# Merging all stages of a gated convolution and attention kernel by a list scheduler in its source

## The chip, the cores and the metric

The kernel runs on one core of one Trainium2 chip. The metric is the time on the device in microseconds (us), from the first to the last instruction of the core. A core has TensorE for matrix products (PE in the profile, with its weight loads as a row of their own, PEld), VectorE (DVE), ScalarE (ACT), GpSimd (POOL), a queue that mostly starts transfers (SP), and 16 DMA engines. TensorE writes only to PSUM, an accumulator memory of 128 partitions with 8 banks of 512 fp32 columns each; VectorE or ScalarE has to carry every result from there to the on-chip working memory. Below, this is called an eviction.

## The reference

There are two branches over the same input x of 2048 positions and 640 channels, mixed by one gate per position. Branch A is a short causal convolution of k with 4 taps, multiplied by v, and then a causal convolution as long as the sequence, done with Fourier transforms. Branch B is an attention in which each position looks at itself and at seven earlier ones, two positions apart; 32 heads have 20 channels each.

```python
x = A_q
g = _sigmoid((x * gate_w).sum(-1, keepdims=True))

# branch A
for t in range(4):
    k_shift = k_shift + k_pad[:, t:t + S, :] * shift_k[:, 3 - t]
kv = k_shift * v
y = irfft(rfft(pad(kv)) * rfft(pad(ssm_k)))[:S]       # length 2 * S
y = y + kv * ssm_D
a = x * y

# branch B
q, k, v = split_heads(x @ wqkv)                       # 32 heads of 20
idx = pos[:, None] - 2 * arange(8)[None, :]           # window of 8, dilation 2
attn = softmax(where(idx >= 0, q . k[idx] * scale, -1e9))
b = (attn @ v[idx]) @ wo

out = g * a + (1 - g) * b
```

All inputs and the output are bf16. The transform is written as matrix products in two steps forward (`s1`, `s2`), a product of spectra, and two steps backward (`i1`, and `i2` with the table T).

## The kernel before

The stages stand one after another in the source, with hand-written interleaving: each stage is a generator, and the main loop advances one or another of them by so many steps. Each stage opens PSUM pools of its own.

In the head x is transposed, v is projected, and VectorE computes the short convolution. Its result goes to a scratch tensor in DRAM, because it is computed with 16 consecutive positions in each partition and the transform needs another layout.

```python
def load_kv(c):
    ...
    if c == 0:
        nc.gpsimd.memset(kh[0:1, 0:3, :], 0.0)
        nc.sync.dma_start(kh[1:128, 0:3, :], raw(k2, 13 * D, [[16 * D, 127], [D, 3], [1, D]]))
    eng.dma_start(kh[:, 3:7, :], raw(k2, t0 * D, [[16 * D, 128], [D, 4], [1, D]]))
    eng.dma_start(vn[:, t0:t0 + 4, :], raw(v2, t0 * D, [[16 * D, 128], [D, 4], [1, D]]))
...
load_x(0); load_w(2); load_x(1)
...
load_kv(0)
load_x(2); load_x(3)
load_w(0); load_w(1)
load_kv(1)
...
            nc.gpsimd.dma_start(raw(kvs, 4 * c * 80, [[16 * 80, 128], [S * 80, 8], [1, 320]]),
                                pr[:, 2].rearrange("p (u m) -> p u m", u=8))
```

The projections of q and k are evicted to a staging tile `stg`, and small transfers ("fragments") of 4 to 20 partitions each sort their rows into the sets of four heads (`qb`, `kb`) that attention uses. There are three sets, used in turn.

Attention runs over 8 groups of four heads, each in 10 halves: scores (`sc`), exp on ScalarE into one of six tiles `ET`, product with v (`O`), division on VectorE. The rest of the projection, and then the transform of the filter for the first three of five channel groups, are slotted in.

```python
for s in range(len(halves)):
    if s + 1 < len(halves):
        scores(s + 1)
    ...
    if 6 <= s < 36:
        advance(qk, 1)
    if s == 20:
        load_h()
    if s == 37:
        ...
        hg = h_early()
    if hg is not None and s % 5 != 4:
        advance(hg, 1)
    advance(kvg, 1)
    pv(s)
kv = p0.tile([128, 2, 64, 80], BF, name="kv", tag="Kslot")
... # kv is read back from its scratch in DRAM
```

Then come the transform of kv, the remaining filter groups, the spectral products, the first inverse step, and, between them, the output projection of attention. Each block of it is scaled by 1 - g and written to a second scratch tensor, which is read back in the layout of the last step:

```python
            for n0, n1 in ((0, 512), (512, 640)):
                for ft in range(NDT):
                    nc.tensor.matmul(opf[:, n0:n1], lhsT=oT[:, ft, :], rhs=wo[:, ft, n0:n1], ...)
            ... # fin = (1 - g) * op, on ScalarE or VectorE
            for r0, n, dst in pos_rows(b_scr, BP * b, BP):
                nc.gpsimd.dma_start(dst, fin[r0:r0 + n, :])
...
    if k == 60:
        qg = p0.tile([128, 16, D], BF, name="qg", tag="Hslot")
        ... # q is loaded
        bl = p0.tile([128, 16, D], BF, name="bl", tag="Kslot")
        ... # b_scr is read back
T = p2.tile([128, 64, 2, 32], BF, name="T", tag="Am", bufs=2)
nc.sync.dma_start(T[:], cf["T"].ap().rearrange("p (a r b) -> p a r b", a=64, r=2))
for t in range(16):
    nc.vector.tensor_scalar(qg[:, t, :], qg[:, t, :], g_nat[:, t:t + 1], None, ALU.mult)
for t0 in range(0, 16, 3):
    ... # i2 = last inverse step on TensorE
    ... # qg = i2 * qg, four parts; qg = qg + bl; qg is stored
```

Of the kernel before, what the change touches and what calls it, by code (L numbers as in the profile page):

```python
# [31 lines left out]
NT = 8  # L32
KW = 128 * NB
QW = BP * NB
GROUPS = [[0, 1, 2, 3], [4, 5, 6, 7], [8, 9, 10], [11, 12, 13], [14, 15, 16]]

# [65 lines left out]
def pos_rows(x2, p0, n):  # L102
    out = []
    for par in range(2):
        a, b = max(p0, HS * par), min(p0 + n, HS * par + S // 2)
        if a < b:
            v = x2.rearrange("(e two) d -> two e d", two=2)
            out.append((a - p0, b - a, v[par, a - HS * par:b - HS * par, :]))
    return out


class Load:
    def __init__(self, nc):
        self.nc = nc
        self.t = dict(a=0.0, d=0.0)

    def pick(self, n):
        ca, cd = n * 0.833 + 80, n * 1.042 + 70
        if self.t["a"] + ca <= self.t["d"] + cd:
            self.t["a"] += ca  # L120
            return "a"
        self.t["d"] += cd
        return "d"

    def copy(self, dst, src, n, eng=None):
        eng = eng or self.pick(n)
        if eng == "a":
            self.nc.scalar.copy(dst, src)  # L128
        else:
            self.nc.vector.tensor_copy(dst, src)  # L130


def advance(gen, n):
    for _ in range(n):
        if next(gen, "end") == "end":
            return False
    return True
# [3 lines left out]
def kernel(  # L141
# [18 lines left out]
    dpool = ctx.enter_context(tc.tile_pool(name="scratch_dram", bufs=1, space=DRAM))  # L160
    b_scr = dpool.tile([S, D], BF, name="b_scr")
    kv_scr = dpool.tile([8, S, 80], BF, name="kv_scr")
    g_scr = dpool.tile([S], F32, name="g_scr")
    cf = {k: nc.inline_tensor(v, name=f"cf_{k}") for k, v in fft_consts().items()}
    ca = {k: nc.inline_tensor(v, name=f"ca_{k}") for k, v in attn_consts().items()}
    ld = Load(nc)
# [3 lines left out]

    p0 = ctx.enter_context(tc.tile_pool(name="p0", bufs=1))
    ident = p0.tile([128, 128], BF, name="ident")
    xS = p0.tile([128, 16, D], BF, name="xS", tag="A")
    vn = p0.tile([128, 16, D], BF, name="vn", tag="Hslot")
# [3 lines left out]
    g_sb = p0.tile([128, 16], F32, name="g_sb")  # L178
    g_nat = p0.tile([128, 16], F32, name="g_nat")
    omg = p0.tile([128, NB], F32, name="omg")  # L180
    oTs = []
    for e in range(3):
        oTb = p0.tile([128, NDT, 128], BF, name=f"oT{e}")
        oTs.append(oTb)

    sA = ExitStack()
    pA = sA.enter_context(tc.tile_pool(name="pA", bufs=1, side="right", reuse_waits="tile"))
    VWs = [p0.tile([128, NB, H // 2, 21], BF, name="VWa", tag="VWa"), pA.tile([128, NB, H // 2, 21], BF, name="VWb")]
    valid = pA.tile([128, NB], BF, name="valid")
    ksets, qsets, ETs = [], [], []  # L190
    for e in range(3):
        kb = pA.tile([128, KW], BF, name=f"kb{e}")
        qb = pA.tile([128, QW], BF, name=f"qb{e}")
        ksets.append(kb); qsets.append(qb)
    NET = 6
    for e in range(NET):
        ETb = pA.tile([128, 2, 512], BF, name=f"ET{e}")
        ETs.append(ETb)
    sB = ExitStack()
    p1 = sB.enter_context(tc.tile_pool(name="pB", bufs=1, side="right", reuse_waits="tile"))  # L200
    sC = ExitStack()
    pC = sC.enter_context(tc.tile_pool(name="pC", bufs=1, side="left", reuse_waits="tile"))
    xT = pC.tile([128, NDT, XW], BF, name="xT")
    W = pC.tile([128, NDT, 3, D], BF, name="W")
    wg = pC.tile([128, NDT], BF, name="wg")
    wl = pC.tile([128, 4, D], BF, name="wl")

# [3 lines left out]
    khs = [None] * 4  # L211

    def load_x(c):
        nc.sync.dma_start(xS[:, 4 * c:4 * c + 4, :], xq4[:, c // 2, 4 * (c % 2):4 * (c % 2) + 4, :])

    def load_w(w):
        nc.sync.dma_start(W[:, :, w, :], W3[:, :, w, :])

    def load_kv(c):
        kh = p1.tile([128, 7, D], BF, name="kh", tag="kh", bufs=2)  # L220
        khs[c] = kh
        t0 = 4 * c
        eng = nc.sync if c < 2 else nc.gpsimd
        if c == 0:
            nc.gpsimd.memset(kh[0:1, 0:3, :], 0.0)
            nc.sync.dma_start(kh[1:128, 0:3, :], raw(k2, 13 * D, [[16 * D, 127], [D, 3], [1, D]]))
        eng.dma_start(kh[:, 3:7, :], raw(k2, t0 * D, [[16 * D, 128], [D, 4], [1, D]]))
        eng.dma_start(vn[:, t0:t0 + 4, :], raw(v2, t0 * D, [[16 * D, 128], [D, 4], [1, D]]))

    nc.sync.dma_start(ident[:], ca["ident"].ap())  # L230
    for c0, c1 in ((0, PRE), (HS, HS + PRE), (2 * HS, XW)):
        nc.gpsimd.memset(xT[:, :, c0:c1], 0.0)
    load_x(0); load_w(2); load_x(1)
    wraw = p1.tile([128, D, 4], BF, name="wraw", tag="stg", bufs=2)
    nc.gpsimd.dma_start(wraw[:], raw(A_shift_k, 0, [[0, 128], [4, D], [1, 4]]))
    nc.gpsimd.dma_start(valid[:], ca["valid"].ap())
    nc.gpsimd.dma_start(wg[:], gate_w.rearrange("(t p) -> p t", p=128))
    load_kv(0)
    load_x(2); load_x(3)
    load_w(0); load_w(1)  # L240
    load_kv(1)
    nc.gpsimd.memset(Dz[:], 0.0)
    nc.gpsimd.memset(omg[:], 0.0)
    for e in range(NET):
        nc.gpsimd.memset(ETs[e][:], 0.0)
    for e in range(3):
        nc.gpsimd.memset(oTs[e][:], 0.0)
    for e in range(2):
        nc.gpsimd.tensor_copy(VWs[e][:, :, :, DH], valid[:].unsqueeze(2).to_broadcast([128, NB, H // 2]))

    def load_feats(e):
        for h4 in range(4):
            nc.sync.dma_start(ksets[e][32 * h4 + DH:32 * h4 + DH + NF, :], ca["mk"].ap())
            nc.sync.dma_start(qsets[e][32 * h4 + DH:32 * h4 + DH + NF, :], ca["mq"].ap())

    load_feats(0)
    for q in range(4):
        nc.gpsimd.dma_start(Dz[32 * q:32 * q + 1, :], A_ssm_D[160 * q:160 * q + 160].unsqueeze(0))
    nc.gpsimd.dma_start(F1b[:], cf["F1b"].ap())
    nc.gpsimd.dma_start(M[:], cf["M"].ap().rearrange("p (a b) -> p a b", a=2))  # L260


    kvs = kv_scr[:]

    def kv_gen():
        nc.vector.tensor_copy(wl[:], wraw[:].rearrange("p c j -> p j c"))
        pr = p0.tile([128, 4, 4 * D], BF, name="pr", tag="Kslot")
        yield
        for c in range(4):
            kh = khs[c]  # L270
            if c:
                nc.vector.tensor_copy(kh[:, 0:3, :], khs[c - 1][:, 4:7, :])
            for j in (0, 1, 3, 2):
                nc.vector.tensor_tensor(pr[:, j].rearrange("p (n c) -> p n c", n=4), kh[:, 3 - j:7 - j, :],  # L274
                                        wl[:, j, :].unsqueeze(1).to_broadcast([128, 4, D]), ALU.mult)
                yield
            nc.vector.tensor_tensor(pr[:, 0:2], pr[:, 0:2], pr[:, 2:4], ALU.add)
            yield
            nc.vector.tensor_tensor(pr[:, 0], pr[:, 0], pr[:, 1], ALU.add)
            nc.vector.tensor_tensor(pr[:, 2].rearrange("p (u n i) -> p n u i", u=8, n=4),  # L280
                                    pr[:, 0].rearrange("p (n u i) -> p n u i", n=4, u=8),
                                    vn[:, 4 * c:4 * c + 4, :].rearrange("p n (u i) -> p n u i", u=8), ALU.mult)
            nc.gpsimd.dma_start(raw(kvs, 4 * c * 80, [[16 * 80, 128], [S * 80, 8], [1, 320]]),
                                pr[:, 2].rearrange("p (u m) -> p u m", u=8))
            if c < 2:
                load_kv(c + 2)
            yield

    kvg = kv_gen()


    pv_ = ExitStack()
    ppv = pv_.enter_context(tc.tile_pool(name="ppv", bufs=2, space=PSUM, reuse_waits="tile"))

    def transposes(c):
        for d0 in (0, 2, 4):
            nd = min(2, NDT - d0)
            tr = ppv.tile([128, 2, 4, 128], BF, name="trx", tag="trx")
            for dd in range(nd):
                for k in range(4):  # L300
                    nc.tensor.transpose(tr[:, dd, k, :], xS[:, 4 * c + k, 128 * (d0 + dd):128 * (d0 + dd) + 128], ident[:, :])  # L301
            ld.copy(xT[:, d0:d0 + nd, ccol(4 * c):ccol(4 * c) + 512],
                    tr[:, 0:nd].rearrange("p d k c -> p d (k c)"), 512 * nd, eng="a")

    def vproj(b):
        ps = ppv.tile([128, 1024], F32, name="psv", tag="psv")
        for n0, n1 in ((0, 512), (512, 640)):
            for dt in range(NDT):
# [28 lines left out]
    def qk_gen(engs):  # L337
        for ft in range(NDT):
            for which in range(2):
                stg = p1.tile([128, KW], BF, name="stg", tag="kh" if ft >= 2 and which else "stg", bufs=2)  # L340
                wd = BP if which == 0 else 128
                for c in range(5):
# [12 lines left out]
                    if c < 4:  # L355
                        yield
# [358 lines left out]
```

The softmax here doesn't subtract the row's maximum and nothing guards it: scores larger than these inputs give would overflow.

## Time and profile before

| | |
|---|---|
| median of three runs | 355.84 us (353.16 to 358.53) |
| span of the profiled execution | 354.1 us |
| busy: PE, DVE, ACT, POOL | 254.6, 211.4, 165.9, 41.2 us |
| first score, last product of attention | 86 us, 212 us |
| last matmul of the first inverse step | 318.8 us |
| first matmul of the last step | 329.9 us |
| moved by DMA | 46.37 MB, mean 131 GB/s |

A line of groups or of the timeline names the line of the source, the engine, the operation and the tiles, as output<-input, with a time in us and the number of instructions. What stands in brackets in the timeline is how long the engine was idle before, and whom it waited for. A line of the chain of waits gives a start, a length and what filled it. A line of the windows view gives, for a stretch of the span, its length, the busy time of PE, PEld, DVE, ACT and POOL with the number of instructions, the granted clock of TensorE as a share of full speed, the share in which the DMA engines were busy, and GB/s. A DMA on the SP queue is shown by the time of its issue; when it landed is seen in who waited for it.

### The profile page before, as it was taken

To read this page: it belongs to the slowest core of one execution; us is meant where nothing else is said; L and a number is where in the kernel's file an instruction comes from. 1 tells how busy PE (TensorE), PEld (TensorE's weight loads), DVE (VectorE), ACT (ScalarE), POOL (GpSimd) and SP (SyncE) were. 2 spreads that over 40 slices of the span, in tenths; PEclk is the share of its full clock that TensorE was granted. 3 is DMA by queue.
4 is the path that set the end of the run, shared out by engine and by line. 5 is a ranking of instruction groups with operands and counts; after the bars stand their busy time and mean duration, and the time that the engine had idled before them with its cause. 6 is when DMAs were issued, how large, how long until landed. Compare 5 with 4: busy or idle time off the path is not lost. (4 is left out here: it accounts for less than half of the span.)

```text
span 354.1 us, 9846 instructions
## 1 busy us (share of the span) xinstructions
PE 254.6 (72%) x4355; PEld 174.0 (49%) x4355; DVE 211.4 (60%) x295; ACT 165.9 (47%) x239; POOL 41.2 (12%) x67
## 2 busy tenths in 40 slices
PE   2760599958779999857877888898989488660430
PEld 2330355524336655545655655575657477660320
DVE  1400999692836565857776633844574668671595
ACT  3250264525526555634545585756565577531000
POOL 8910023010150000000000000112111000000000
PEclk9995599999659999755555556999999968867555
DMA  7375854974441499761891019217121507999165
GB/s 200 137 241 178 267 151 118 211 199 102 103 84 31 88 168 163 193 191 30 181 213 51 4 27 217 65 41 170 39 54 38 138 4 164 213 213 212 57 149 132
DMA packets 34603, 46.37 MB, mean 131 GB/s; under 512 B 23757, under 2 KB 28572, under 8 KB 33152
## 3 DMA queue, kind: packets, MB, share of 16 engines
q1 hardware_dynamic: 31088, 35.77, 42.9%
q0 software_dynamic: 2896, 8.66, 9.3%
q10 hardware_dynamic: 576, 1.31, 1.6%
q8 instruction: 34, 0.56, 0.7%
q14 instruction: 9, 0.07, 0.1%
HBM read 27.19 MB, written 7.87 MB: 99 GB/s over the span
## 5 line engine op out<-in xcount | busy, mean ns | idle before, releaser
L421 ACT ACTIVATE ET<-sc 128x726 bf16<-128x726 f32 (+1 forms) x80 | 67.1, 858 | 57.8 <-PE sc L418 57.2
L352 PE MATMUL pj<-xT,W 128*128 128x484 bf16 (+3 forms) x250 | 55.9, 368 | 6.2 <-ACT stg L128 4.0
L274 DVE TENSOR_TENSOR pr<-kh,wl 128x2560 bf16<-128x2560 bf16 x16 | 23.0, 1487 | 28.2 <-DMA kh<-in_A_k_dram 23.4
L485 PE MATMUL s<-Am,G 64*128 64x64 bf16 x1280 | 29.2, 206 | 13.9 <-DVE Hs L130 4.1
L352 PEld LDWEIGHTS <-W 128*128 128x128 bf16 x250 | 21.7, 102 | 29.8 <-issue 11.9
L418 PE MATMUL sc<-qb,kb 31*128 31x121 bf16 x544 | 36.0, 260 | 0.6 <-issue 0.6
L485 PEld LDWEIGHTS <-G 64*128 64x128 bf16 x1280 | 26.1, 105 | 17.9 <-issue 12.1
L435 PEld LDWEIGHTS <-ET 128*128 128x128 bf16 x544 | 22.4, 102 | 20.8 <-ACT ET L421 9.3
L618 PE MATMUL op<-wo,oT 128*128 128x128 bf16 (+1 forms) x170 | 27.3, 310 | 4.3 <-ACT oT L128 3.5
L130 DVE CAST stg<-pj 128x484 bf16<-128x484 f32 (+3 forms) x30 | 17.9, 598 | 20.8 <-PE pj L352 16.2
L130 DVE CAST Am<-s 128x512 bf16<-128x512 f32 x36 | 23.4, 686 | 11.5 <-PE s L468 9.9
L309 PE MATMUL psv<-W,xT 128*128 128x128 bf16 (+1 forms) x170 | 27.6, 327 | 2.8 <-DMA W<-in_B_wqkv_dram 2.8
L525 PE MATMUL i<-M,Hw 128*128 128x128 bf16 x160 | 25.6, 253 | 4.9 <-DVE Hw L513 2.6
L525 PE MATMUL i<-M,Hs 128*128 128x128 bf16 x160 | 26.0, 253 | 4.1 <-DVE Hs L512 4.1
L626 POOL DMA_DIRECT2D b_scr<-fin x18 | 9.6, 531 | 161.7 <-DVE fin L624 137.9
L128 ACT CAST Am<-s 128x512 bf16<-128x512 f32 x44 | 23.6, 610 | 6.7 <-PE s L468 4.6
L525 PEld LDWEIGHTS <-Hs 128*128 128x128 bf16 x160 | 22.5, 154 | 7.0 <-DVE Hs L512 4.5
L130 DVE CAST Hs<-s 128x1024 bf16<-128x1024 f32 x15 | 18.4, 1224 | 11.7 <-PE s L485 11.7
L301 PE MATMUL trx<-ident,xS 128*128 128x128 bf16 x80 | 7.9, 265 | 22.6 <-DMA xS<-in_A_q_dram 20.4
L525 PEld LDWEIGHTS <-Hw 128*128 128x128 bf16 x160 | 22.4, 155 | 3.0 <-DVE Hw L513 3.0
L128 ACT CAST Cm<-i 128x1024 bf16<-128x1024 f32 x15 | 15.2, 1012 | 15.9 <-PE i L525 15.7
L309 PEld LDWEIGHTS <-xT 128*128 128x128 bf16 x170 | 14.7, 106 | 15.4 <-issue 7.2
(73 smaller groups left out, 362.5 us busy)
## 6 DMA issues: line engine op xcount, KB each, us to landing
Hw<-Hs SPq DMA_DIRECT2D x10, 512.0 KB
xS<-in_A_q_dram SPq DMA_DIRECT2D x4, 640.0 KB
kv_scr<-pr POOLq DMA_DIRECT2D x4, 640.0 KB, 5.4
h_lin<-in_A_ssm_k_dram SPq DMA_DIRECT2D x8, 320.0 KB
kv<-kv_scr SPq DMA_DIRECT2D x4, 640.0 KB
qg<-in_A_q_dram SPq DMA_DIRECT2D x4, 640.0 KB
bl<-b_scr SPq DMA_DIRECT2D x4, 640.0 KB
W<-in_B_wqkv_dram SPq DMA_DIRECT2D x3, 800.0 KB
```

The costliest lines, as they stand in the source:

```text
L128: self.nc.scalar.copy(dst, src)
L130: self.nc.vector.tensor_copy(dst, src)
L274: nc.vector.tensor_tensor(pr[:, j].rearrange("p (n c) -> p n c", n=4), kh[:, 3 - j:7 - j, :], wl[:, j, :].unsqueeze(1).to_broadcast([128, ...
L309: nc.tensor.matmul(ps[:, n0:n1], lhsT=xT[:, dt, BP * b:BP * b + 128], rhs=W[:, dt, 2, n0:n1], start=(dt == 0), stop=(dt == NDT - 1))
L352: nc.tensor.matmul(ps[:, 0:n], lhsT=W[:, dt, which, 128 * ft:128 * ft + 128], rhs=rhs, start=(dt == 0), stop=(dt == NDT - 1))
L418: nc.tensor.matmul(sc[:, hh, BP * bb:BP * bb + BP], lhsT=kb[r:r + DH + NF, 128 * b:128 * b + 128], rhs=qb[r:r + DH + NF, BP * b:BP * b + B ...
L421: nc.scalar.activation(ETs[s % NET][:, :, 0:nw], sc[:, :, 0:nw], ACT.Exp, scale=SCALE)
L435: nc.tensor.matmul(O[:, sl * 21:sl * 21 + 21], lhsT=ET[:, hh, BP * bb:BP * bb + 128], rhs=VWs[t // 4][:, b, 4 * (t % 4) + 2 * hf + hh, :], ...
L485: nc.tensor.matmul(o, lhsT=st["G"][rows, j, r, :], rhs=Am[rows, 2 * j + r, :, :], start=(r == 0), stop=(r == 1), tile_position=(64 * c, 0) ...
L525: nc.tensor.matmul(o, lhsT=src[:, c, :, :, 8 * oc + il].rearrange("p q j -> p (q j)"), rhs=M[:, k, :], start=(k == 0), stop=(k == 1), skip ...
L618: nc.tensor.matmul(opf[:, n0:n1], lhsT=oT[:, ft, :], rhs=wo[:, ft, n0:n1], start=(ft == 0), stop=(ft == NDT - 1))
L626: nc.gpsimd.dma_start(dst, fin[r0:r0 + n, :])
```

## The change

The interleaving by hand is replaced by a list scheduler that runs while the kernel is built. Each stage is a stream that yields requests: which engines may do it, a guessed duration, what it depends on, how many PSUM slots it takes or gives back. The scheduler picks the request that can start earliest, with a small penalty by priority, books it, and lets the stream emit its instructions. What is built is one fixed order for each engine. All stages share one ring of four PSUM slots of two banks each. An eviction that either ScalarE or VectorE may do goes to the one that would be done first.

Both scratch tensors for data go. k and v are loaded with 160 channels of 64 positions a partition, which is the layout of the transform, so kv never leaves the chip. The output projection multiplies weight tiles of 32 positions, so that its result comes out in the layout of the last step and stays on chip. The product of q with the gate moves from VectorE to GpSimd, and q and T are loaded as soon as their places are free. The core of the diff:

```diff
-class Load:
-    def pick(self, n):
...
+class Plan:
+    def start(self, r, e):
+        t = self.at[e]
+        for d in r.deps:
+            if d.t is None:
+                return INF
+            t = max(t, d.t + LAT.get((d.eng, e), 60.0))
+        if r.take:
+            free = sorted(s.free.t + 120.0 if s.free.t is not None else INF for s in self.slots)
+            t = max(t, free[r.take - 1])
...
+    def run(self):
+        while self.streams:
+            for k, (pri, gen, r) in enumerate(self.streams):
+                end, st, e = self.best(r)
...
+                key = (st + 120.0 * p, p, k)
...
-    b_scr = dpool.tile([S, D], BF, name="b_scr")
-    kv_scr = dpool.tile([8, S, 80], BF, name="kv_scr")
+    plan = Plan(4)
...
+        def load_kv(a):        # after load_x(0), Wv, load_x(1..3)
+            dk = [ev(f"conv{a - 2}")] if a >= 2 else []
+            dv = [ev(f"conv{a - 1}")] if a >= 1 else []
+            for q in range(4):
+                yield from load(f"k{a}{q}", kin[a % 2][32 * q:32 * q + 32, lo:19, :],
+                                raw(k2, n0 * D + 160 * q, [[64 * D, 32], [D, 19 - lo], [1, 160]]), ...)
...
+        for q in range(4):
+            nc.gpsimd.dma_start(kin[0][32 * q + 1:32 * q + 32, 0:3, :],
+                                raw(k2, 61 * D + 160 * q, [[64 * D, 31], [D, 3], [1, 160]]))
...
+            nc.vector.tensor_tensor(kv[:, :, 16 * a:16 * a + 16, :].rearrange("p c n i -> p n c i"),
+                                    pa[:].rearrange("p n (c i) -> p n c i", c=2),
+                                    vin.rearrange("p n (c i) -> p n c i", c=2), ALU.mult)
...
-                stg = p1.tile([128, KW], BF, name="stg", tag="kh" if ft >= 2 and which else "stg", bufs=2)
+                stg = pL.tile([128, KW], BF, name="stg", tag=f"stg{w}")
...
-    NET = 6
+    NET = 8
...
+        for t in range(16):
+            g = yield Req("P", 5 * (215.0 + 56.0), [last], take=1)
+            op = psum(g, "op", (128, 1024))
+            for ft in range(NDT):
+                for n0, n1 in ((0, 512), (512, 640)):
+                    for gg in range(4):
+                        nc.tensor.matmul(op[32 * gg:32 * gg + 32, n0:n1],
+                                         lhsT=raw(a, HS * (t % 2) + t // 2 + 8 * gg, [a.ap[0], [32, 32]]),
+                                         rhs=wo[:, ft, n0:n1], ..., tile_position=(0, 32 * gg))
+            ... # bl[:, t, :] = (1 - g) * op
...
+    def late_loads():
+        yield Req("S", 1.0, [ev("us1")])        # last s1 of the transform of kv
+        ... # q is loaded
+        r = yield Req("S", 60.0, [ev("i10")], move=us(1048576, 8192))
+        nc.sync.dma_start(st["T"][:], cf["T"].ap().rearrange("p (a r b) -> p a r b", a=64, r=2))
...
+    def qscale():
+        for t in range(16):
+            r = yield Req("G", 800.0, [ev("qg"), ev("gate")])
+            nc.gpsimd.tensor_scalar(qg[:, t, :], qg[:, t, :], g_nat[:, t:t + 1], None, ALU.mult)
```

The short convolution now runs in four chunks of 8 operations over 2560 elements (four products with a tap, three sums, the product with v). The fragment transfers stay on the SP queue; the constant feature rows of the sets are loaded on GpSimd's.

## The prediction

> **What bounds the kernel now.** I read the busy line first, to see whether one engine fills the span.
>
> ```profile
> PE 254.6 (72%) x4355; PEld 174.0 (49%) x4355; DVE 211.4 (60%) x295; ACT 165.9 (47%) x239; POOL 41.2 (12%) x67
> ```
>
> TensorE is the fullest, but about 100 us of the span have no matmul in them. The second view, busy time by stretch, says where. I cut at the first score (86 us), the last attention product (212), the end of the first inverse step (320) and the first matmul of the last step (330):
>
> ```profile
> 0.00:86.00 86.00, 56.40 (x432) 32.50 (x435) 47.47 (x31) 33.05 (x67) 24.78 (x39) 0.88 0.65 184
> 86.00:212.00 126.00, 104.28 (x1725) 68.70 (x1726) 78.14 (x149) 67.57 (x82) 6.84 (x10) 0.68 0.51 108
> 212.00:320.00 108.00, 86.68 (x1695) 67.79 (x1691) 67.10 (x86) 65.22 (x91) 9.55 (x18) 0.89 0.51 115
> 320.00:330.00 10.00, 0.06 (x16) 0.06 (x16) 0.09 (x1) 0.06 (x1) 0.00 (x0) 0.68 0.75 184
> 330.00:354.00 24.00, 7.22 (x512) 4.94 (x512) 18.60 (x30) 0.00 (x0) 0.00 (x0) 0.50 0.45 112
> ```
>
> The columns are length, busy PE, PEld, DVE, ACT, POOL, then clock, DMA share and GB/s. PE stands still for 30 us in the head, 22 in attention, 21 in the transforms, 10 waiting, and 17 in the last step. For the end I read the chain in order of time:
>
> ```profile
> 295.13 10.32 DMA qg<-in_A_q_dram
> ...
> 305.52 24.38 DMA T<-cf_T
> 329.90 0.04 issue
> 329.94 1.25 PE i L673 x93
> ```
>
> 35 us of the chain are loads issued only at 295: q, the attention result read back from DRAM, and the table T, 6.3 MB at 206 GB/s (DMA view of 300 to 330). The last inverse matmul ended at 318.8, so 11 us of this are exposed. After it VectorE is the wall: the chain of the last step is its products and sums, 350.0 minus 331.2 = 19 us.
>
> For the head I read the timeline:
>
> ```profile
> 4.14 13.27 SPq L227 DMA_DIRECT2D kh<-in_A_k_dram  x1
> ...
> 35.84 5.70 DVE L274 TENSOR_TENSOR pr<-kh,wl 128x2560 bf16<-128x2560 bf16 x4 [23.18 <-DMA kh<-in_A_k_dram]
> ...
> 39.05 1.89 PE L301 MATMUL trx<-ident,xS 128*128 128x128 bf16 x16 [14.89 <-DMA xS<-in_A_q_dram]
> ```
>
> The issuing queue is stuck for 13.3 us in the k load, so the second half of x arrives late and PE idles 14.9 us. In attention the largest wait is ACT for scores, 57.2 us in total: ScalarE is not the limit there; PE, at a granted clock of 0.68 and 83% busy, is.
>
> **What the Trainium skill says.** "DMA: Bandwidth & Descriptors", section "Why a DMA increments its semaphore by 16 and not by 1": a copy is spread over the largest number of engines up to 16 that divides the slowest dimension, so 127 partitions land on one engine. The trace agrees: the 127-partition load of k's three earlier rows (L226) stands right before the 13.27 us jam. "TensorE: Matmul & The Clock Gate", section "Part 3: Packing small matmuls — row/col tiling": column tiles run concurrently, three of 32 columns gave 2.38x. The kernel before tiles rows and columns only in its last step, 512 matmuls in 7.3 us of busy time, which agrees that small tiles overlap; columns alone no run shows. "GPSIMD Engine Reference", section "3.1 Elementwise — side-by-side cycle accounting": one-input work costs 1.03 to 1.8 cycles per element. "SBUF — State Buffer", section "Who interferes with whom": VectorE with two SBUF inputs excludes a GpSimd instruction that reads SBUF. The trace before has no such pair running together.
>
> **The change, part by part.** The costs written in the scheduler's source only set an order; I use none of them as times. The durations below are from the groups by shape, the counts from the emitted order.
>
> *Total work hardly moves.* PE: the same columns for projection, scores, products and transforms; the output projection becomes 640 matmuls of 32 columns instead of 170 of 128. With the skill's 2.38x for three tiles I take about 3x for four (estimate), so 16 x 5 x 4 pairs of 512 and 128 columns cost about 28 us, against 27.3 now. DVE: the convolution becomes 32 operations of 2560 elements, 32 x 1.487 = 48 (now 23.0+11.3+5.9+6.0+2.0 = 48); the wide weight copy shrinks from 5.3 to 1.3; normalising 8 x 2.8 = 22 (now 27); the 16 gate products (4.8) leave; 36 transform evictions x 1.22 = 44, 14 of the projection 11, 20 spectral products 24, oT 6.5, xT 4.6, last step 20. Sum 182, now 211. ACT: exp 67, 64 transform evictions x 1.02 = 65, projection 13, V 12, gated output 16 x 0.79 = 13, small 5: 175, now 166. No engine passes PE's 250 or so. So the gain must come from idle time.
>
> *Head.* The bad load becomes four of 31 partitions on GpSimd's queue, and x comes whole before k. 3.4 MB of x and the V weights, then 1.3 MB of k and v, at the 210 GB/s that even 128-byte pieces reached (DMA view of 124 to 142): 4.75 / 0.210 = 23, plus 2.5 to begin, so 25 us. Convolution chunk 0 runs 25 to 37, chunk 1 to 49. The query projection of the first 128 features alternates with V blocks on PE (1.1 + 1.6 us), starts at about 30 when its weights land, and is evicted at about 43; the keys' part at about 54. The 14 fragment copies cost 1 us of issue each (7.30 us for 7 before), the last 7 run 54 to 61 and land at about 64. PE by then has 56.6 us of work behind it. First score: 66, now 86. Gain 20.
>
> *Attention.* Work in it: 165 projection matmuls x 0.236 = 39, scores 36, products 27.4, 64 + 96 transform matmuls 7, together 109; the same groups summed to 119 before for 104 of union, so 109 x 0.876 = 96 of PE. It had 22 idle. One ring of four slots and 8 exp buffers instead of 6 should help, but a single staging tile per operand instead of two, and the 2.1 MB of G and 2.6 of the filter put ahead of later fragments (10 + 13 us of queue), should cost. I leave 16 idle: 112 us, ending at 178. Now 126; gain 14.
>
> *Transforms.* More lies here than before, since the filter transform is moved out of attention: 1184 second-step matmuls x 0.019 = 22, 256 first-step x 0.059 = 15, inverse 27, transposes 8, output 28 = 100; with the same overlap (91.9 of groups gave 86.7) 95 of PE. ACT has 77 and DVE 64 in it, so ACT is no wall but is close. Before 21 of 108 were idle; better merging gives me 12: 107, ending at 285. Gain about 1, for more work.
>
> *End.* q is loaded once the last forward first step is done, T behind it; the read-back of b is gone. 2.6 + 1.0 MB at 206 GB/s are 17 us plus 2; from that point to the end of inversion took 21 us before (298 to 319), so the loads just hide. GpSimd's gate: 640 elements x 1.03 to 1.8 cycles at 1.2 GHz are 0.55 to 0.96 us a row (estimate), three rows under 3 us, against 3.4 of VectorE for three rows: hidden, apart from contention, for which I add 3. The last step stays 24: 1 + 24 + 3 = 28. Now 34. Gain 6.
>
> Sum: 66 + 112 + 107 + 28 = 313 us, a gain of some 41 against the profile's 354.
>
> **Rivals.** One: a new wait in place of the old. The order is frozen in the source by guessed durations, and ACT and DVE take instructions in order; a staging eviction that waits for late fragments blocks exps behind it. For it: the attention clock of 0.68, and 50 us of fragment issues. Against it: before, the same waits were 4 us each. This would give 325 to 340. Two: the column-tiled projection does not overlap its weight loads; at one after the other, 80 x 4 x 0.34 = 109 us instead of 28, about 380. Against it is the last step's own behaviour. Three: PE becomes dense and the clock stays high. The clock was 1.00 from 220 to 280; with attention near 0.85, the 96 us shrink toward 80: 295. Four: GpSimd's rows cost over 2 us, or the two engines lock each other out; then 16 rows x 2 set the end, plus 10: 323.
>
> **Range and chances.** Rival one is the likeliest deviation, three gives the low end: 292 to 338 holds eight in ten. Slower needs rival two, or several at once. Faster by over 2%: 0.91, within 2%: 0.05, slower: 0.04.
>
> **What would show it.** First score between 62 and 72; no wait of PE for x over 5 us; last attention product near 178; no DMA link of over 3 us in the chain's last 40 us; the first final matmul within 2 us of the last Cm eviction; a final step of 24 to 27. Wrong would be: the op group above 45 us of PE; ACT waiting on fragments for over 15 us in attention; VectorE waiting on GpSimd in the last step.

## The result, and the profile after

| | before | changed kernel |
|---|---|---|
| time, median | 354.88 us (353.16 to 358.53) | 313.47 us (311.70 to 314.45) |
| ratio | | 0.8836, 95% interval 0.8783 to 0.8889 |
| span of the profiled execution | 354.1 us | 312.3 us |

The predicted 313.0 us was met, but not every term of its sum was. The stages, cut at the same events in both profiles, show where the 41.8 us came from:

| stage | before | after | difference | predicted length |
|---|---|---|---|---|
| head, to the first score | 86.0 | 65.2 | -20.8 | 66 |
| attention, to the last product with V | 125.6 | 107.9 | -17.7 | 112 |
| transforms, to the first matmul of the last step | 118.3 | 103.7 | -14.6 | 107 |
| last step | 24.2 | 35.5 | +11.3 | 28 |

The 118.3 us of before hold 11.1 us of waiting for T. The prediction cut the last two stages at the last matmul of the first inverse step; cut there, they are 102.4 and 36.8 us long. Three stages shrank, and the last one grew by half. Attention and transforms belong together, because most of the filter's transform that stood in attention now stands in the transforms (480 of its matmuls in attention before, 160 after). TensorE stood idle for 52.9 of their 243.9 us before and for 30.8 of their 211.6 us after. The busy line on the page of the changed kernel:

```profile
PE 236.8 (76%) x4820; PEld 166.3 (53%) x4825; DVE 177.4 (57%) x195; ACT 166.4 (53%) x198; POOL 71.4 (23%) x84
```

VectorE lost 34 us of work, 4.8 of it the gate product, and GpSimd gained 30, as much as the gate product takes there. TensorE's busy time fell by 18 us, so the shorter span is not less idle time alone. Its granted clock is higher in the mean (0.83 against 0.78), and its matmuls overlap more: the 544 of the scores took 260 and 256 ns each, but filled 36.0 us before and 29.1 after. No run separates the two. Next the busy time by stretch, columns as in the prediction's table:

```profile
0.00:65.00 65.00, 48.90 (x410) 29.68 (x415) 40.98 (x30) 22.43 (x30) 36.83 (x61) 0.95 1.07 193
65.00:173.00 108.00, 90.92 (x1410) 55.55 (x1411) 55.20 (x79) 70.18 (x89) 4.77 (x7) 0.72 0.48 101
173.00:277.00 104.00, 90.10 (x2527) 76.31 (x2524) 62.03 (x57) 73.78 (x80) 2.23 (x2) 0.95 0.39 89
277.00:312.00 35.00, 6.92 (x512) 4.77 (x479) 19.23 (x30) 0.00 (x0) 27.55 (x15) 0.59 0.32 77
```

In the last row VectorE works 19.23 us of 35, and GpSimd 27.55: the wall of the last step has changed its engine. The chain in order of time says the same, from the landing of q on:

```profile
258.75 15.81 DMA qg<-in_A_q_dram
...
274.77 9.33 POOL qg L793 x5
284.10 1.86 POOLq L880
285.96 16.74 POOL qg L793 x9
302.72 2.36 DVE qg L819 x4
```

The group on the page gives the price of one row:

```profile
L793 POOL TENSOR_SCALAR qg<-qg,g_nat 128x640 bf16<-128x640 bf16 x16 | 29.8, 1873 | 165.5 <-PE i L728 165.5
```

1873 ns a row, 16 rows in series, first start 274.77. (The releaser printed here is a matmul; the chain shows that q landed last.) How long VectorE waited for these rows (in total, times, longest), and the same rows as VectorE did them in the kernel before:

```profile
DVE qg L819 <- POOL qg L793: 15.8, 5, 7.9
```

```profile
L663 DVE TENSOR_SCALAR qg<-qg,g_nat 128x640 bf16<-128x640 bf16 x16 | 4.8, 383 | 2.1 <-DMA qg<-in_A_q_dram 2.1
```

In the head the timeline now reads, for the transposes of x, the first operation of the convolution and the first score:

```profile
5.72 2.31 PE L413 MATMUL trx<-ident,xS 128*128 128x128 bf16 x20 [5.72 <-DMA xS<-in_A_q_dram]
...
23.37 1.49 DVE L389 TENSOR_TENSOR pa<-kvin,wl 128x2560 bf16<-128x2560 bf16 x1 [2.46 <-DMA kvin<-in_A_k_dram]
...
65.15 0.26 PE L537 MATMUL sc<-qb,kb 31*128 31x121 bf16 x1 [4.67 <-issue]
```

PE waits for x once, at the very start (5.7 us), and VectorE's first product waits 2.5 us for k where it waited 23.2. A weak spot is left in attention. The timeline of the issuing queue and of TensorE's and ScalarE's work on the same stretch:

```profile
84.56 20.53 SPq L312 DMA_DIRECT2D h_lin<-in_A_ssm_k_dram  x8
106.65 0.58 SPq L513 DMA_DIRECT2D kb<-stg  x1
...
99.31 0.52 PE L537 MATMUL sc<-qb,kb 31*128 31x121 bf16 x12 [0.51 <-DVE oS L583]
101.61 6.69 PE L479 MATMUL pj<-xT,Wqk 128*128 128x384 bf16 x25
...
112.54 1.01 ACT L234 CAST stg<-pj 128x1024 bf16<-128x1024 f32 x1 [11.18 <-DMA qb<-stg]
...
121.04 0.42 PE L537 MATMUL sc<-qb,kb 31*128 31x121 bf16 x16
```

Eight filter loads hold the queue for 20.5 us, the last key fragment of a batch leaves after them (a batch is the 7 or 8 fragments of one block of 128 features), ScalarE waits 11.2 us for staging to come free, and no score is computed for 21 us (99.8 to 121.0; the texts below say 18). PE fills 14 of them with projections.

### The profile page after: what moved, and what is told of

Its sections match the earlier page's. It is cut to its first block, busy times and chain, and to the rows that moved or that the text cites. A ratio compares the mean times of both kernels' runs of the same rounds, so it can differ in the third digit from the quotient of the medians.

```text
span 312.3 us, 10653 instructions
## 1 busy us (share of the span) xinstructions
PE 236.8 (76%) x4820; PEld 166.3 (53%) x4825; DVE 177.4 (57%) x195; ACT 166.4 (53%) x198; POOL 71.4 (23%) x84
## 4 chain that ended last, share of the span: by engine, by line
PE 46%; SPq 13%; DMA 12%; POOL 8%; ACT 7%; DVE 6%; issue 4%; POOLq 1%; ACTq 0%
PE pj L479 13%; POOL qg L793 8%; SPq L312 8%; PE op L767 7%; PE s L618 5%; DMA qg<-in_A_q_dram 5%; PE sc L537 4%; PE i L728 4%; SPq L513 4%; ACT ET L544 4%; PE O L569 4%; DMA qb<-stg 4%; PE psv L428 3%; PE s L600 3%; DMA Wqk<-in_B_wqkv_dram 2%
## 5 line engine op out<-in xcount | busy, mean ns | idle before, releaser
L544 ACT ACTIVATE ET<-sc 128x726 bf16<-128x726 f32 (+1 forms) x80 | 63.6, 863 | 21.3 <-PE sc L537 20.8
L793 POOL TENSOR_SCALAR qg<-qg,g_nat 128x640 bf16<-128x640 bf16 x16 | 29.8, 1873 | 165.5 <-PE i L728 165.5
L479 PE MATMUL pj<-xT,Wqk 128*128 128x363 bf16 (+3 forms) x250 | 58.9, 388 | 7.4 <-DVE stg L236 5.3
L479 PEld LDWEIGHTS <-Wqk 128*128 128x128 bf16 x250 | 25.3, 108 | 31.1 <-issue 15.2
L537 PE MATMUL sc<-qb,kb 31*128 31x121 bf16 x544 | 29.1, 256 | 12.7 <-ACT ET L544 4.7
L234 ACT CAST Am<-s 128x1024 bf16<-128x1024 f32 x32 | 31.4, 1021 | 5.2 <-PE s L600 5.0
L537 PEld LDWEIGHTS <-kb 31*128 31x128 bf16 x544 | 16.6, 107 | 26.1 <-issue 20.8
L234 ACT CAST stg<-pj 128x968 bf16<-128x968 f32 (+5 forms) x16 | 12.7, 807 | 31.1 <-DMA qb<-stg 13.4
L428 PE MATMUL psv<-Wv,xT 128*128 128x512 bf16 (+1 forms) x165 | 27.4, 314 | 1.2 <-DVE xT L236 1.0
L236 DVE CAST stg<-pj 128x726 bf16<-128x726 f32 (+4 forms) x14 | 11.3, 810 | 25.1 <-DMA qb<-stg 12.2
L767 PE MATMUL op<-wo,oT 128*32 128x512 bf16 (+1 forms) x640 | 25.4, 304 | 0.0
L711 DVE TENSOR_TENSOR Hs<-Up,Hs 128x2048 bf16<-128x2048 bf16 x10 | 12.2, 1221 | 21.1 <-ACT Up L234 21.0
L234 ACT CAST VW<-psv 128x640 bf16<-128x640 f32 x17 | 11.8, 697 | 20.8 <-PE psv L428 20.8
```

The source lines that it names most:

```text
L428: nc.tensor.matmul(ps[:, n0:n1], lhsT=xT[:, dt, BP * b:BP * b + 128], rhs=Wv[:, dt, n0:n1], start=(dt == 0), stop=(dt == NDT - 1))
L479: nc.tensor.matmul(ps[:, i, 0:n], lhsT=Wqk[:, dt, w, 128 * ft:128 * ft + 128], rhs=rhs, start=(dt == 0), stop=(dt == NDT - 1))
L537: nc.tensor.matmul(sc[:, hh, BP * bb:BP * bb + BP], lhsT=kb[r:r + DH + NF, 128 * b:128 * b + 128], rhs=qb[r:r + DH + NF, BP * b:BP * b + B ...
L544: nc.scalar.activation(ETs[e][:, :, 0:nw], sc[:, :, 0:nw], ACT.Exp, scale=SCALE)
L767: nc.tensor.matmul(op[32 * gg:32 * gg + 32, n0:n1], lhsT=raw(a, HS * (t % 2) + t // 2 + 8 * gg, [a.ap[0], [32, 32]]), rhs=wo[:, ft, n0:n1] ...
L793: nc.gpsimd.tensor_scalar(qg[:, t, :], qg[:, t, :], g_nat[:, t:t + 1], None, ALU.mult)
```

## The experiments

Each kernel was timed in three rounds beside the kernel before on the same chip. Kernels are compared by their ratios to it; a difference in us is the difference of two ratios times 355, good to 3 or 4 us. Ratios are taken over undisturbed executions alone, medians over all of a kernel's, so a median can lie a little off its ratio, and the profiles of three runs (gate on ScalarE, filter loads on GpSimd's queue, ScalarE gate with other guesses) are of executions 1 to 2.5% longer than the rest. The first score alone falls between 62.5 and 68.5 us in profiles of the changed kernel and of those that change nothing ahead of it, so a stage is known to a few us only. The changed kernel is at 0.8836.

| run | median us | ratio | interval | against |
|---|---|---|---|---|
| gate on ScalarE | 302.64 | 0.8466 | 0.8389 to 0.8544 | changed: -13 us |
| q early | 308.98 | 0.8645 | 0.8547 to 0.8742 | changed: -7 |
| filter loads on GpSimd's queue | 316.96 | 0.8814 | 0.8734 to 0.8893 | changed: -1 |
| three slots | 340.63 | 0.9582 | 0.9521 to 0.9644 | changed: +26 |
| before, load split | 338.75 | 0.9471 | 0.9399 to 0.9544 | before: -19 |
| kv by DRAM | 324.75 | 0.9049 | 0.8966 to 0.9132 | changed: +8 |
| b by DRAM | 314.30 | 0.8770 | 0.8700 to 0.8840 | changed: -2 |
| filter loads late | 312.15 | 0.8732 | 0.8667 to 0.8796 | changed: -4 |
| slots dealt out | 336.40 | 0.9433 | 0.9344 to 0.9522 | changed: +21 |
| ScalarE gate, other guesses | 307.68 | 0.8592 | 0.8532 to 0.8652 | ScalarE gate: +4 |
| ScalarE gate, filter late | 302.12 | 0.8410 | 0.8330 to 0.8490 | ScalarE gate: -2 |
| slots dealt out, filter late | 324.94 | 0.9160 | 0.9111 to 0.9209 | filter late: +15 |

### The last step: who applies the gate, and when

```diff
-            r = yield Req("G", 800.0, [ev("qg"), ev("gate")])
-            nc.gpsimd.tensor_scalar(qg[:, t, :], qg[:, t, :], g_nat[:, t:t + 1], None, ALU.mult)
+            r = yield Req("A", 720.0, [ev("qg"), ev("gate"), ev("Cm")])
+            nc.scalar.activation(qg[:, t, :], qg[:, t, :], ACT.Copy, scale=g_nat[:, t:t + 1])
```

> The 16 row products of q with the gate move from GpSimd to ScalarE, booked after the last inverse eviction; q is still loaded late, at the same point. Theory A (the last step lasts 35.5 us because GpSimd needs 1.87 us a row, 16 rows in series from the landing of q): ScalarE needs about 0.7 us a row, VectorE then waits for nothing but its own 19.2 us, the last step falls to about 27 us and the whole to about 305 us (-8). Rival B (the wall of the last step is VectorE or the write of the output, GpSimd only the name of the last waiter): at most -2 us. Rival C (q's late landing is what matters, whoever applies the gate): the first product still waits, but only some 2 us after the first final matmul, so C alone also gives only -1 to -3.

The last stretch of this run, and its gate group by shape:

```profile
277.50:303.00 25.50, 6.96 (x512) 4.86 (x512) 18.70 (x30) 11.57 (x16) 0.00 (x0) 0.63 0.43 105
```

```profile
L793 ACT ACTIVATE qg<-qg,g_nat 128x640 bf16<-128x640 bf16 x16 | 11.8, 816 | 2.7 <-issue 2.7
```

The last step fell from 35.5 to 25.5 us. The stages before it kept their length (107.8 and 103.6), so all of the gain is here (10 us in this stage, 11 for the whole by the medians, 13 by the ratios). Theory A stands, B and C fall: a row costs ScalarE 816 ns, and VectorE, with 18.7 us of work in 25.5, is the wall again.

```diff
-        yield Req("S", 1.0, [ev("us1")])
-        qg = p0.tile([128, 16, D], BF, name="qg", tag="kv")
+        for k in range(3):              # rows 0-5, 6-11, 12-15
+            yield Req("S", 1.0, [ev(f"i1{k + 1}")])
+            qt = st["p2"].tile([128, 4096], BF, name="qg", tag=f"Hs{k + 1}")
-            r = yield Req("G", 800.0, [ev("qg"), ev("gate")])
+            r = yield Req("G", 1870.0, [ev(f"qg{t // 6}"), ev("gate")])
```

> q is loaded in three parts of 6, 6 and 4 rows, each as soon as a spent filter-spectrum buffer is free, so it lands some 8 to 25 us before the last inverse eviction; the gate stays on GpSimd at whatever it costs there. Theory A: rows done early take the slow engine off the end; the last step falls to 25 to 27 us, the whole to about 304 us (-9), with the GpSimd rows still at 1.87 us each, since the price belongs to the instruction. Rival D (1.87 us is the price of contention with VectorE): the rows would change their length with VectorE's load; idle VectorE below 1.5 us, busy above 2. Rival E: the earlier load and the gate, put beside the busiest part of the transforms, slow VectorE's own operations and give back 3 us or more: 308 or above.

The last step fell to 24.2 us, a little below what A said, but the transforms grew from 103.7 to 111.6, and with 308.98 us for the whole E's sign came: 7 us were gained instead of 9. D has a part. First the rows by their tile in this run (count, then ns minimum, median, maximum):

```profile
L797 POOL TENSOR_SCALAR qg<-qg,g_nat x16: 1877/1882/3993, 250.2 to 288.5; 128x640 bf16<-128x640 bf16 x16
```

Then GpSimd's first row in the timeline, and VectorE's beside it:

```profile
250.21 3.29 POOL L797 TENSOR_SCALAR qg<-qg,g_nat 128x640 bf16<-128x640 bf16 x1 [142.90 <-DMA qg<-in_A_q_dram]
...
250.61 1.22 DVE L714 TENSOR_TENSOR Hw<-Up,Hw 128x2048 bf16<-128x2048 bf16 x1
251.74 1.74 DVE L711 TENSOR_TENSOR Hs<-Up,Hs 128x2048 bf16<-128x2048 bf16 x1
```

1.88 us is the price of a row by itself. Rows that meet the spectral products took 2.87 to 3.99 us, and a product beside them 1.74 instead of 1.22. This adds some 6 us to GpSimd's sum (36.0 against 29.8) and under 2 to VectorE's. The rest of the longer transforms goes with the new order, since the scheduler had planned anew; which step of it costs, this run doesn't tell.

### The head: one load

```diff
-            nc.sync.dma_start(kh[1:128, 0:3, :], raw(k2, 13 * D, [[16 * D, 127], [D, 3], [1, D]]))
+            nc.sync.dma_start(kh[1:113, 0:3, :], raw(k2, 13 * D, [[16 * D, 112], [D, 3], [1, D]]))
+            nc.sync.dma_start(kh[113:128, 0:3, :], raw(k2, (13 + 16 * 112) * D, [[16 * D, 15], [D, 3], [1, D]]))
```

> This is the kernel before with one edit: its load of k's three earlier rows over 127 partitions is split into 112 and 15 partitions. Theory A (most of the head's gain of 20 us is that load, which went out through one DMA engine and held the queue for 13.3 us, so x came late): k and x arrive some 13 us sooner, PE's wait of 14.9 us for x nearly goes, the first score moves from 86 to 73-76 us and the whole falls by 8 to 13 us, to about 343-347. Rival (the head is paced by its 6 MB of loads and the convolution, or by the new order of the loads, and the jam only moved bytes around): first score within 3 us of 86, whole within 3 us of 355.

The timeline of the kernel before with this edit:

```profile
2.81 1.58 SPq L226 DMA_DIRECT2D kh<-in_A_k_dram  x1
4.99 0.36 SPq L228 DMA_DIRECT2D kh<-in_A_k_dram  x1
...
16.27 5.70 DVE L275 TENSOR_TENSOR pr<-kh,wl 128x2560 bf16<-128x2560 bf16 x4 [3.60 <-DMA kh<-in_A_k_dram]
```

```profile
0.00:70.30 70.30, 54.01 (x432) 30.99 (x434) 47.34 (x31) 32.95 (x67) 24.83 (x39) 0.95 0.79 225
```

The load that was stuck for 13.27 us (now L228) leaves in 0.36 us, the convolution starts at 16 instead of 36, and the first score is at 70.3. The gain of 19 us is even above the expected 8 to 13. Attention and transforms kept their lengths (125.2 and 117.0). So 15.7 of the 20.8 us that the changed kernel wins in the head need no scheduler at all: splitting one load does it. The DMA view of the kernel before shows why. Its line for the queue, from 13.0 to 17.4 us (packets, MB, share of the 16 engines):

```profile
q1 hardware_dynamic: 30, 0.12, 6.4%
```

While the queue is stuck, one engine's worth of the sixteen works (1/16 is 6.3%), and the kernel moves 26 GB/s.

### Attention: the slots

```diff
-    plan = Plan(4)
+    plan = Plan(3)
```

> The list scheduler gets three PSUM slots of two banks instead of four and plans everything again. Theory A (the gain over the kernel before in attention and transforms is what one common ring gives, since matmuls of any stage fill the gaps while evictions run): with a quarter of it gone PE idles more, 4 to 12 us slower, spread over both stages. Rival H (the gain comes from the head's loads and the kept intermediates, the ring hardly counts): within 2 us. A loss above 20 us would say that the evictions, not PE, pace the stages.

Attention grew to 129.2, the transforms to 111.9. A holds in direction, but the loss is over twice what it allowed, and the count of slots and the sharing are mixed up in it. That evictions pace the stages, as the text has it for a loss above 20 us, does not follow either: a stall for a transfer, found next, is in this run too. The next kernel keeps four and takes away the sharing while attention lasts:

```diff
+        if not self.private:            # from the first score to the last product with V
+            return self.slots
+        return {1: self.slots[0:2], 2: self.slots[2:3], 3: self.slots[3:4]}[r.kind]
```

> The four PSUM slots of the changed kernel are dealt out while attention lasts, much as the kernel before had them: two slots for scores, one for the products with V, one for everything else (projections and transforms). The count of slots stays four and the scheduler plans again. The run with three common slots lost 27 us. Theory A (it is the sharing that pays in attention: any stage takes the slot that comes free next): attention grows from 108 us to 118-128, the transforms stay within 3 us of 104, the whole comes to 323-335. Rival J (the loss with three slots came from their number; with four, private or common is the same, and the attention stage gained by its 8 exp buffers and the order): attention within 4 us of 108, whole within 4 us of 313.

Attention is 123.8 us, close to the 125.6 of before. That looks like A. But the timeline of this run shows a second thing:

```profile
81.28 22.45 SPq L319 DMA_DIRECT2D h_lin<-in_A_ssm_k_dram  x8
...
105.38 5.21 SPq L520 DMA_DIRECT2D kb<-stg  x7
...
110.89 0.96 PE L545 MATMUL sc<-qb,kb 31*128 31x121 bf16 x16 [14.27 <-DMA kb<-stg]
113.95 1.23 DVE L243 CAST stg<-pj 128x1024 bf16<-128x1024 f32 x1 [26.64 <-DMA qb<-stg]
```

All seven key fragments of a batch stand behind the filter loads; in the changed kernel six of them leave at 79.5, before those. VectorE loses 26.6 us there, and PE 14.3. With three slots the same waits are 26.7 and 18.0 us. So slots and loads had to be told apart.

### Attention: the filter loads

```diff
-            nc.sync.dma_start(dst, src)
+            (nc.gpsimd if name[0] == "h" else nc.sync).dma_start(dst, src)
```

> Only the eight filter loads are issued from GpSimd's queue instead of SyncE's; the order of every compute engine stays the same. Theory A (the hole of 18 us in the scores of the attention stage comes from fragment transfers standing behind 20.5 us of issuing of the filter loads on one queue): the waits of ScalarE and VectorE for fragments fall from 13 and 12 us to some 4 each, the attention stage shortens by 4 to 10 us, and as the frozen order lets some of it be lost later the whole gains 3 to 8 us. Rival F (it is the single staging tile per operand, refilled only after the former fragments left, whatever the queue): the waits stay within 3 us of what they are and the whole within 2 us. Rival G (the transfer itself, 2.6 MB of 128-byte pieces, shares the DMA engines with the fragments): waits halve at most, gain 1 to 3.

The waits for fragments fell (VectorE's for query fragments from 12.2 us to 4.9, ScalarE's of 13.4 is gone from the list), and nothing was gained (-1 us). Theory A fell: other waits grew in their place, for projections to evict (VectorE from 9.6 to 11.5 us, ScalarE from 3.7 to 8.2), while the order stayed the same. The next eight query fragments are issued from 93.2 to 112.8, 19.6 us against 6.3 in the changed kernel. But some 9 us of that are pauses in which the queue waits for scores and, by the profile, for the output weights to land; one issue took 4.8 us by itself. How much the DMA engines hold back is not shown apart.

```diff
-  [[64, 32], [S, 80], [1, 64]]), 327680, 128, [ev("conv3")])
+  [[64, 32], [S, 80], [1, 64]]), 327680, 128, [ev("conv3"), ev("set3")])
```

> The filter loads and the output weights wait until the fourth fragment set is out, and the scheduler plans again; everything else as in the changed kernel. The run with the filter loads on GpSimd's queue cut the waits of ScalarE and VectorE for fragments but gained nothing; there the same 2.6 MB still shared the DMA engines with the fragments. Theory G (the transfer, not the queue, delays the fragments, and the 18 us without scores cost time): with fragments first the hole closes, attention ends 4 to 8 us sooner, the whole gains 3 to 7 us. Rival I (PE's queue is paced by its own work at a clock of 0.72 and fills the hole with projections, so moving the hole moves nothing): attention within 3 us of 108, whole within 3 us of 313.

Scores run on through 103 to 117, but the hole did not close, it moved. The loads now leave in front of the batches after the fourth set, and these stand behind them in turn:

```profile
106.92 13.09 SPq L312 DMA_DIRECT2D h_lin<-in_A_ssm_k_dram  x8
...
130.07 0.97 ACT L234 CAST stg<-pj 128x968 bf16<-128x968 f32 x1 [11.05 <-DMA kb<-stg]
131.10 0.66 PE L537 MATMUL sc<-qb,kb 31*128 31x121 bf16 x8 [6.99 <-DVE stg L236]
```

From 117.6 to 131.1 only eight score matmuls run, and PE idles 7.0 us (5.3 in the changed kernel's hole). Attention went from 107.9 to 105.5 us, the whole gained 4 us with an uncertainty of 3. Between G and I this does not decide: no run takes the loads out of attention altogether. The two edits together tell more about the slots:

> The dealt-out slots again, now with the filter loads held back until the fourth fragment set is out. Both runs with fewer usable slots (three common ones, or four dealt out) lost 23 to 27 us, and both show one stall of VectorE for fragments of 26.7 us, because there a whole batch of key fragments, which in the changed kernel goes out just ahead of the filter loads, fell in behind their 20 us on the queue. Theory L (the slots matter only through that accident of order): without the filter loads in the way the private slots cost under 5 us, so 312 to 318. Theory A (sharing pays by itself, as the pool that is full holds PE back): still 10 to 23 us slower than the same loads with common slots (312.15), so 322 to 335. Between 318 and 322 both have a part.

Attention and transforms of this run, and below those with the same loads and common slots:

```profile
64.90:176.60 111.70, 85.71 (x1333) 51.49 (x1333) 47.86 (x72) 73.80 (x92) 4.77 (x7) 0.79 0.46 98
176.60:284.60 108.00, 93.70 (x2571) 79.99 (x2568) 64.22 (x58) 75.94 (x82) 3.40 (x2) 0.92 0.38 86
```

```profile
68.50:174.00 105.50, 86.95 (x1451) 54.58 (x1452) 58.57 (x82) 69.23 (x88) 4.78 (x7) 0.78 0.49 104
174.00:276.10 102.10, 89.64 (x2465) 76.21 (x2462) 60.71 (x55) 73.25 (x79) 2.06 (x2) 0.94 0.39 91
```

Holding the loads back takes 12 us off attention with dealt-out slots (123.8 to 111.7), but only 2.4 with common ones. What is left to sharing is 6.2 us in attention and 5.9 in the transforms, which inherit some hundred matmuls of the filter's transform that common slots had let into attention's gaps (1451 against 1333). So with 15 us by the times, theory A stands by its own range, and the accident of order adds some 6 us by the times (21 against 15), 10 in attention. Two reservations: the two profiled executions differ by 7.2 us only, since the head and the last step were 4.9 us shorter with dealt-out slots; and each plan has its own waits for transfers. With dealt-out slots PE waits 12.6 us for key fragments (6.3 of them behind the filter loads), with common ones 7.0 us behind the loads. How much of the 12 us is sharing and how much the new order is therefore not shown.

### The intermediates

```diff
+        nc.gpsimd.dma_start(kv_scr[:], kv[:].rearrange("p c n i -> p (c n i)"))     # after conv3
+        nc.sync.dma_start(kv[:].rearrange("p c n i -> p (c n i)"), kv_scr[:])       # after set7
```

> The changed kernel with kv (2.6 MB) written to DRAM after the fourth convolution chunk and read back when the last fragment set is done, before its forward transform, as the kernel before did with its intermediate. Theory A (keeping kv on chip takes transfers out of time that had DMA room: the share of DMA in attention is 0.48, in the transforms 0.39): between 0 and +6 us, the read of some 12.5 us hiding behind the filter's transform. Rival (the round trip was a real part of the gain, since the forward transform of kv waits for its return and the write stands in the way of the fragments): +8 to +20 us.

It cost 8 us, at the lower edge of the rival's range. Not the return: the transforms stayed near (104.8). Attention grew from 107.9 to 114.3 and its DMA share from 0.48 to 0.58; there the write runs beside the filter loads and the fragments, and the weights of a score waited 4.8 us for it:

```profile
PEld L541 <- DMA kv_scr<-kv: 4.8, 1, 4.8
```

```diff
+            nc.gpsimd.dma_start(b_scr[:, t, :], bl[:, t, :])                          # each row
+            nc.sync.dma_start(bl[32 * g:32 * g + 32], b_scr[32 * g:32 * g + 32])      # before the last step
```

> The changed kernel with the gated attention output (2.6 MB) written to DRAM row by row and read back once all 16 rows are written, before the last step. Theory A (before, it was the read-back of b in one queue with q and T that stood exposed ahead of the last step): the read-back takes 12.5 us of the queue from about 247 us on, q lands some 4 to 12 us later than at 275, and GpSimd's gate, which starts when q lands, moves the end by as much: +4 to +12 us. Rival (the end is set by the gate alone and the read-back fits into the idle DMA time between 246 and 259): within 2 us.

No loss: the rival holds. The scheduler put q and T ahead of the read-back, so q landed at 272.6, and the waits of the last step were:

```profile
DVE qg L829 <- DMA bl<-b_scr: 5.5, 1, 5.5
DVE qg L826 <- POOL qg L800: 2.0, 1, 2.0
```

The first sum waits 5.5 us for b, behind which GpSimd's rows go on; the gate, not b, still sets the end. With a fast gate this would not be free.

### Two tries at a better version

```diff
-  g = yield Req("P", 51.0 * nb + 30.0, [ev(f"set{t}")], take=1)            # scores
+  g = yield Req("P", 104.0 * nb + 60.0, [ev(f"set{t}")], take=1)
-  g = yield Req("P", 27.0 * 4 * ntot, deps + [ev("VW")], take=1)           # products with V
+  g = yield Req("P", 36.0 * 4 * ntot, deps + [ev("VW")], take=1)
```

> The gate on ScalarE as in the first experiment, and the two most mistaken guesses of the scheduler, 51 ns a block for scores and 27 ns a head and block for the products with V, set to 104 and 36, the size seen in the trace. Theory A (the order is frozen by guesses, so better ones should make fewer stalls): 2 to 5 us below the 302.6 of the gate on ScalarE alone. Rival K (the guesses only set a priority among streams, and PE is over 80% busy in attention anyway): within 2 us of 302.6, either side.

Truer guesses made it 4 us slower, with an uncertainty of as much. In the new order all seven key fragments of a batch stand behind the filter loads again, and VectorE waits:

```profile
DVE stg L236 <- DMA qb<-stg: 28.8, 1, 28.8
```

Theory A falls, and K is not right either: the guesses matter, as far as this run shows, through where they happen to put a fragment transfer in the queue. No run tries a truer model of the transfers, so how much that would bring stays open.

The ScalarE gate and the late filter loads (the two diffs above) together:

> The gate on ScalarE together with the filter loads after the fourth fragment set. If the two act in different stages they add up: 302.6 minus the 1.3 us that the later filter loads brought alone, so 300 to 303. If the later filter loads only gained by an earlier landing of q that GpSimd's gate then used, nothing adds: 302 to 304.

302.12 us, ratio 0.8410: the last step 25.6 us as with the gate alone, attention 106.1. The 2 us against the gate alone are within the uncertainty. Both are about 15% below the kernel before.

## Why the prediction was right, and where it was not

**Head: right in size and cause.** 65.2 against 66; convolution chunks at 23.4 to 35.4 and 37.7 to 49.8 against 25 to 37 and 37 to 49. After the first load of x PE never waits for x. The load split confirms the cause that the prediction named, the load over 127 partitions: with 112 and 15 the queue runs free, and before, one sixteenth of the DMA engines was at work.

**Attention: right, 4 us too cautious.** 91 us of PE against 96, and 17 idle against 16. Most of the 17.7 us is therefore work moved out and done denser, not idle time filled (22 before). The eight exp tiles, the choice of engine for an eviction and the clock were not tested apart. The clock rose only to 0.72 (rival three, 0.85, did not come). Rival one came in part: ScalarE waits 17.1 us for fragments (13.4 for query, 3.7 for key fragments), over the 15 named as a sign of being wrong, but PE had projections to do meanwhile. It is the dealt-out run that shows how close this was to a stall of 26.6 us.

**Transforms: right, 3 us too cautious.** 90 us of PE against 95, idle 14 against 12. The column-tiled projection is 25.4 us of PE (busy time of that tile in the stage) against 28 estimated. Four column tiles do run side by side; rival two fell.

**End: wrong by 7.5 us (8.8 by the prediction's own cut), which the other terms paid.** That 313 was met to half a us is luck: 8 us of caution in the other stages stood against this. The loads were right: q takes 19.7 us from its issue at 255.05 to 274.77, the last inverse matmul ends at 275.5, so they just hide. The step that failed is "three rows under 3 us, against 3.4 of VectorE for three rows: hidden". Three rows take 5.6. The term was 0.55 to 0.96 us a row, worked out from the 1.03 to 1.8 cycles that the prediction took from the Trainium skill, "GPSIMD Engine Reference", section "3.1 Elementwise — side-by-side cycle accounting". The section calls 1.8 the best case of a tight loop; the prediction took it for the upper end. The trace says 1.873 us, twice that, and where the two differ the measurement decides. VectorE's wait for GpSimd, named as a sign of being wrong, is 15.8 us. VectorE had done the same 16 rows in 4.8 us before, 0.38 each and partly overlapping. Rival four, at "16 rows x 2", described the rows to within 2 us (29.8), but not the total of 323.

**The 3 us for contention: in the wrong place.** In the last step itself the sums beside GpSimd took 1212 ns against 1158 with the gate on ScalarE, 0.3 us over all, and the rows no longer than 1.885. The exclusion that the Trainium skill describes in "SBUF — State Buffer", section "Who interferes with whom", shows only where the spectral products run back to back with the gate, as in the run with q early. Why the sum, with two operands in on-chip memory as well, hardly does it, stays open.

## What to carry to other kernels

Look at the loads before rewriting the schedule: of 41 us, 16 lay in one transfer whose 127 partitions could be split by hand, and a change of a line shows it. A shared pool of accumulator slots can pay as much by letting a later stage's work slip into the gaps of this one as in this stage itself (5.9 and 6.2 us here), but an order frozen from guesses is only as good as its guess of when transfers leave the queue; measure the longest wait for a transfer after every new plan. Before an elementwise product goes to an idle engine, compare the price of a row there, times the rows on the path, with the work it is to hide behind.

## What was not expected of the hardware

- One gate row of 128 x 640 bf16 costs 1.873 us on GpSimd, 0.816 on ScalarE and 0.383 on VectorE; 2.9 ns an element on GpSimd, whatever else ran in the last step.
- GpSimd's row grew to 2.87 to 3.99 us beside VectorE's spectral products, and three of those from 1.22 to 1.74 us, but beside VectorE's sums the rows stayed at 1.87 to 1.89 us and the sums grew from 1.16 to 1.21 only.
- The eight filter loads of 320 KB in 128-byte pieces held their queue for 20.5 us, 2.6 us each; issued after the fourth set's fragments, the same eight took 12.2 and 13.1 us.
